# A mixer kernel's 3389 operations in a written-out order, in place of one derived from a list of priorities

## The chip, the cores and the metric

The program runs on one core of a Trainium2 chip. A core has a matmul engine (TensorE, PE in the profile, with its weight loads shown apart as PEld), three engines that work on tiles element by element (VectorE = DVE, ScalarE = ACT, GpSimd = POOL), and SyncE (SP), which here only issues transfers (DMAs). Each engine works through its own queue in order; engines wait for each other by semaphores. The metric is the device time of one execution in microseconds, lower being better; for each kernel the median of several runs.

## What is computed

Two kinds of layers alternate, A, B, A, B, over x of 2048 rows and 512 columns. The same weights serve both rounds.

```python
def _A_ref(x, wqkv, wo):                     # H = 32 heads of 16, window W = 8, dilation 2
    q, k, v = split(x @ wqkv)                # heads
    idx = pos[:, None] - off[None, :]        # off = 0, 2, ..., 14
    logits = einsum("bhsd,bhswd->bhsw", q, k[idx]) * scale     # idx < 0 masked
    o = einsum("bhsw,bhswd->bhsd", softmax(logits), v[idx])
    return merge(o) @ wo

def _B_ref(x, w1, w2, w3, w4):
    h = gelu(layernorm(x) @ w1)              # 512 -> 512
    hs = shift(h) @ w2                       # quarters of h shifted by +1, -1, +2, -2 rows
    x1 = x + hs
    return x1 + gelu(layernorm(x1) @ w3) @ w4        # 512 -> 1792 -> 512

x = x + _A_ref(layernorm(x), wqkv, wo)
x = x + _B_ref(layernorm(x), w1, w2, w3, w4)
x = x + _A_ref(layernorm(x), wqkv, wo)
x = x + _B_ref(layernorm(x), w1, w2, w3, w4)
```

## The kernel before

The 2048 rows are cut into four blocks of 512, each of four tiles of 128 rows; n = 0 to 7 counts the blocks of the first round (0 to 3) and of the second (4 to 7). For each n there are five stages:

- `p1_stream(n)` (for n = 0 `p1_quarters`) normalizes each tile, turns it (rows to columns, by `turn_pe`, four PE transposes, or `turn_dma`, one DMA transpose) and multiplies it with wqkv: per tile three blocks of 12 matmuls, whose results ACT copies to `ev` and SP stores to memory (`q_d`, `kv_d`).
- `p2(n)` is the attention in four units `qt` of eight heads. SP loads `q` and `kv` for it (unit n = 0 gets them by copies on the chip); DVE multiplies, reduces and adds the products (`prod`), POOL takes some of the additions.
- `p3(n)` multiplies with wo, adds to the residual tile `xs` (loaded by `load_res`), normalizes, turns, and multiplies with w1 (four blocks of 12), whose GELU goes to `h`.
- `p4(n)` multiplies with w2, adds, normalizes and turns again.
- `p5(n)` runs 14 chunks of the wide layer: w3 up to `mm`, GELU, w4 down into four accumulators `acc`. From n = 1 on each chunk loads a w3 and a w4 tile of 256 KB from memory into one of eight buffers `w`.

A matrix product is computed from 16-bit halves: each f32 operand is split into a high part (ACT, or POOL) and a rest (DVE), and three products are summed (`HLS`). The weights are scaled by a power of two from their sum of squares: `small_weight` does so for wo, w1 and w2 (load, a square on ACT, a small matmul with `ones` in `power_of`, a power on POOL), and `big_pair(c)` for a pair of chunks of w3 and w4, whose split halves are stored in memory for `p5`.

The program writes none of its instructions directly. Each step is an operation of a graph (`Graph.__call__`), made with the engines that may run it (`alts`: most have one, some two, such as DVE or POOL), planned durations, the buffers that it reads and writes, and the operations that must come before. An operation has a number, in the order in which it is made; `#2462` below is the operation with number 2462. At the end `plan` (line 265) puts all operations in one order, picks the engine of those that have a choice, and gives each buffer one of the places of its kind (`slots`: eight `w`, three `kv`, four `mm`, and so on). Then every operation is issued in this order, and `InOrder` keeps each engine's instructions in it. All instructions pass through one helper, so every row of the profile names line 385; rows are told apart by the names of tiles.

Before, `plan` is a simulation with a clock `now`. Whenever an engine is free, it starts the ready operation with the lowest key for which buffers are free:

```python
for e in (PE, ACT, DVE, POOL, SP):
    if free[e] > now or not ready[e]:
        continue
    ...
        it = heapq.heappop(ready[e])
        ...
        if all(sum(1 for s in pool[k] if s[0] <= now) >= m for k, m in need.items()):
            got = o
```

The key is the operation's entry in the list `PLACES`. An operation with two engines goes to the one that comes to it first.

## Time and profile before

| | |
|---|---|
| median of 3 runs | 1191.29 us (1185.78 to 1193.92) |
| the profiled execution | 1187.69 us |
| its span, first to last instruction | 1185.9 us |
| PE without an instruction in the span | 40.7 us |
| mean granted PE clock | 0.991 |

Rows of a timeline give the start in us from the span's start, the length, the engine, the operation with the tile written and the tiles read, the shape, the number of instructions merged into the row, and in brackets the engine's idle time before it and what ended it. Rows of stretches give, for each engine, the busy time and the number of instructions, then the granted PE clock, the share of the DMA engines and the GB/s. A matmul of 512 columns is shown as 0.38 us long, but its successor starts after 0.216 us: 12 of them take 2.6 us. `SPq` is SP's queue issuing a transfer; its length is not that of the transfer.

### The profile page before, as it was taken

What the parts mean: (1) busy time and instruction counts of PE and PEld (TensorE: products, weight loads), DVE (VectorE), ACT (ScalarE), POOL (GpSimd) and SP (SyncE); (2) the same over time, 40 slices, a digit from 0 to 9 for tenths busy, and PEclk for the clock granted to TensorE, in tenths of its full rate; (3) what the DMA queues carried; (4) which work ended last, traced back from release to release, by engine and by line L of the source; (5) the groups of instructions that cost most, each with busy time, mean ns of one, the idle gap of its engine ahead of it and who ended that gap; (6) DMA issues with size and microseconds to landing.
All of it is one profiled execution on the core that took longest, in us unless ns stands there. A gap on an engine that the chain in (4) does not pass through costs nothing.

```text
span 1185.9 us, 15311 instructions
## 1 busy us (share of the span) xinstructions
PE 1145.2 (97%) x5270; PEld 543.8 (46%) x5270; DVE 896.4 (76%) x1015; ACT 640.3 (54%) x1121; POOL 419.9 (35%) x568
## 2 busy tenths in 40 slices
PE   8989999999899989999999999999998999999998
PEld 6534444554344444444444444444343444444554
DVE  4789989998789989989877898269987789314122
ACT  5854577326865476555564467354644665445331
POOL 5443445004552345253641265031633352311000
PEclk9989999999999999999999999999999999999999
DMA  7565987877897685975578748578488765335222
GB/s 225 169 191 143 262 212 191 197 187 167 231 261 204 176 202 116 237 189 132 132 199 211 193 112 202 129 179 219 108 205 207 164 135 170 92 88 105 91 93 58
DMA packets 228046, 201.13 MB, mean 170 GB/s; under 512 B 109912, under 2 KB 171352, under 8 KB 227968
## 3 DMA queue, kind: packets, MB, share of 16 engines
q1 hardware_dynamic: 226352, 198.39, 65.3%
q10 hardware_dynamic: 1616, 1.77, 0.5%
q8 instruction: 41, 0.67, 0.2%
q14 instruction: 37, 0.30, 0.1%
HBM read 132.64 MB, written 37.87 MB: 144 GB/s over the span
## 4 chain that ended last, share of the span: by engine, by line
PE 75%; DVE 7%; DMA 7%; ACT 4%; SPq 3%; POOL 2%; issue 2%; DVEq 0%; ACTq 0%; POOLq 0%
PE mm L385 54%; PE acc L385 21%; DVE prod L385 4%; SPq L385 3%; DMA w<-w 2%; DVE L L385 1%; ACT junk L385 1%; POOL c L385 1%; DMA w<-in_B_w_dram 1%; ACT f L385 1%; DMA w<-in_A_x_dram 1%; POOL b L385 1%; DMA kv<-x 1%; DVE f L385 1%; DMA h<-in_B_w_dram 0%
## 5 line engine op out<-in xcount | busy, mean ns | idle before, releaser
L385 PE MATMUL mm<-nT,w 128*128 128x512 f16 (+1 forms) x1288 | 305.1, 390 | 7.9 <-DMA w<-w 4.9
L385 PE MATMUL acc<-w,g 128*128 128x512 f16 (+1 forms) x1260 | 308.2, 395 | 3.1 <-DMA w<-w 3.0
L385 PE MATMUL mm<-wq_hl,xt 128*128 128x512 f16 x1008 | 229.1, 384 | 4.3 <-DVE xt L385 2.2
L385 ACT ACTIVATE mm<-mm,s_w 128x512 f32<-128x512 f32 (+1 forms) x144 | 90.7, 630 | 207.9 <-PE mm L385 207.6
L385 PEld LDWEIGHTS <-w 128*128 128x128 f16 x1344 | 124.9, 98 | 148.3 <-DMA w<-w 6.8
L385 PEld LDWEIGHTS <-g 128*128 128x128 f16 x1176 | 115.4, 98 | 143.4 <-issue 7.3
L385 PEld LDWEIGHTS <-xt 128*128 128x128 f16 x1008 | 99.1, 99 | 124.5 <-issue 6.7
L385 DVE TENSOR_TENSOR prod<-kv,L 128x2048 f32<-128x2048 f32 x64 | 149.7, 2339 | 3.7 <-POOL o L385 1.8
L385 DVE TENSOR_TENSOR prod<-kv,q 128x2048 f32<-128x2048 f32 x58 | 137.8, 2376 | 13.1 <-DMA kv<-kv_d 7.6
L385 DVE TENSOR_REDUCE L<-prod 128x128 f32<-128x2048 f32 x64 | 145.6, 2276 | 0.2
L385 DVE TENSOR_TENSOR prod<-prod 128x1024 f32<-128x1024 f32 (+1 forms) x101 | 108.8, 1077 | 1.5
L385 DVE SCALAR_TENSOR_TENSOR g<-mm,c_g,g 128x512 f16<-128x512 f32 x56 | 41.8, 746 | 78.8 <-ACT g L385 78.7
L385 POOL TENSOR_TENSOR g<-f,g 128x512 f16<-128x512 f32 x32 | 44.0, 1378 | 145.0 <-ACT f L385 73.7
L385 PE MATMUL mm<-nT,w_hl 128*128 128x512 f16 x384 | 86.8, 379 | 5.2 <-ACT junk L385 3.1
L385 PE MATMUL mm<-w_hl,h 128*128 128x512 f16 x384 | 85.8, 379 | 0.0
L385 POOL TENSOR_TENSOR prod<-prod 128x512 f32<-128x512 f32 x33 | 47.3, 1432 | 102.8 <-DVE prod L385 102.6
L385 PE MATMUL mm<-wo_hl,oT 128*128 128x512 f16 x336 | 75.1, 379 | 0.0
L385 ACT ACTIVATE g<-mm,c_g 128x512 f16<-128x512 f32 x98 | 67.2, 686 | 2.1
L385 PEld LDWEIGHTS <-oT 128*128 128x128 f16 x426 | 41.5, 98 | 50.9 <-DVE oT L385 1.7
L385 POOL TENSOR_SCALAR b<-b 128x1 f32<-128x1 f32 (+1 forms) x48 | 22.8, 476 | 117.6 <-ACT junk L385 115.8
L385 ACT ACTIVATE ev<-mm,s_kv 128x512 f32<-128x512 f32 x56 | 38.2, 683 | 48.4 <-PE mm L385 44.6
L385 ACT ACT_TABLE_LOAD x46 | 59.0, 1283 | 4.1 <-issue 3.3
(205 smaller groups left out, 1385.5 us busy)
## 6 DMA issues: line engine op xcount, KB each, us to landing
w<-w SPq DMA_DIRECT2D x196, 256.0 KB
kv<-kv_d SPq DMA_DIRECT2D x112, 352.0 KB
w<-in_B_w_dram SPq DMA_DIRECT2D x56, 256.0 KB
kv_d<-ev SPq DMA_DIRECT2D x112, 128.0 KB
q_d<-ev SPq DMA_DIRECT2D x28, 256.0 KB
w<-g SPq DMA_DIRECT2D x28, 256.0 KB
q<-q_d SPq DMA_DIRECT2D x28, 256.0 KB
x<-x SPq DMA_DIRECT2D x26, 256.0 KB
```

The costliest lines, as they stand in the source:

```text
L385: i = f(*a, **k).ins
```

## The change

`PLACES` is now a permutation that says which place each operation has in one fixed order of all 3389, and a second list, `OTHER`, names the operations that run on the second of their engines. `plan` no longer chooses: it walks through the operations in this order and checks that each comes after those that it needs. It still computes planned times, but only to give a buffer the place that is planned to be free first. Nothing else differs: the operations, their tiles and the numbers of buffers are the same.

```diff
-import heapq
...
 PLACES = [int(k) for k in """
-627 626 619 617 724 832 135 355 315 730 540 1183 440 580 604 607 657 613 795 793 184 624 77 21
...
+103 2 7 0 1 179 3 4 11 10 17 8 18 9 20 25 51 46 36 37 5 6 14 15
...
 """.split()]
 
+OTHER = {int(k): 1 for k in """
+37 100 101 102 103 106 114 118 128 137 165 246 291 339 374 377 378 403 404 408 433 434 437 438
...
+2625 2629 2648 2757 2945 2955 2965 2975 3165
+""".split()}
...
 def plan(ops, slots):
-    free = list(FREE)
+    free, latest = list(FREE), {}
     lane, lanes = 0, [0.0] * LANES
     pool = {k: [(0.0, j) for j in range(len(v))] for k, v in slots.items()}
...
-    while left or fin:
...
-        for e in (PE, ACT, DVE, POOL, SP):
-            if free[e] > now or not ready[e]:
-                continue
...
+    for o in sorted(ops, key=lambda o: o.key):
+        assert o.n == 0, "an operation stands before one that it needs"
+        e, d, o.fn, cls = o.alts[OTHER.get(o.seq, 0)]
+        begin = o.est
+        for b in o.touch:
+            if b.slot is None:
+                got = min(pool[b.kind])
+                pool[b.kind].remove(got)
+                begin, b.slot = max(begin, got[0]), got[1]
+                b.t = slots[b.kind][b.slot]
+        begin = max(begin, free[e])
...
+        order.append(o)
...
+        for b in o.touch:
+            latest[b] = max(latest.get(b, 0.0), o.end)
+            b.left -= 1
+            if b.left == 0:
+                pool[b.kind].append((latest[b] + LAT, b.slot))
     return order
...
-    for _, _, o in plan(op.ops, slots):
+    for o in plan(op.ops, slots):
         o.fn()
```

The operations that the text names, with their new places in the order (lower comes first), are these:

| Engine | number (new place): what it is |
|---|---|
| PE | 494 (195), 90 (212), 497 (220): turn of a tile of `p1_stream(1)`, a block of `p1_quarters`, the first block on that turned tile |
| PE | 329 (243): the small matmul of `big_pair(6)`; 644 (254), 654 (257), 650 (258), 647 (276): turn of a tile of `p1_stream(2)` and its three blocks; 379 (269): turn of the first unit of `p2(0)`; 147 (277): w1's small matmul |
| PE | 1009 (569), 836 (570), 1013 (573): last turn of `p3(0)`, a block of `p1_stream(3)`, the first w1 block |
| PE | 1030 (607), 185 (618): a w1 block of `p3(0)`, the small matmul of `big_pair(0)` |
| PE | 858 (694), 1041 (695): a block of `p1_stream(3)`, the first turn of `p4(0)` |
| PE | 1232 (1127), 1373 (1153), 1237 (1161): last turn of `p4(1)`, a block of `p1_stream(4)`, the first w3 block of `p5(1)` |
| PE | 209 (988), 1352 (1008): the small matmul of `big_pair(1)`, a block of `p1_stream(4)` |
| ACT | 643 (245), 146 (271): normalization before 644, w1's square; 206 (987): a square of `big_pair(1)` |
| SP | 325 (241), 444 (250), 145 (253): a load of `big_pair(6)`, a copy of K for unit 3 of `p2(0)`, the load of w1 |
| SP | 201 (942), 205 (962), 1518 (983): two loads of `big_pair(1)`, a residual tile of `p3(2)` |
| SP | 1552 (1369): the last DMA transpose of `p3(2)` |
| SP | 2462 (2562), 2795 (2738): the w4 tile of chunk 11 of `p5(4)`, the w3 tile of chunk 5 of `p5(5)` |
| DVE | 375 (209): a product of the first unit of `p2(0)` |

Of the operations with a choice, 108 run on another engine than in the trace of before: 49 go from POOL to DVE and 30 from DVE to POOL (additions of `p2` and of the residual in `p4`), 14 from POOL to ACT and 9 from ACT to POOL (high parts and normalizations), 4 from ACT to DVE and 2 from DVE to ACT (squares at the start).

## The prediction

> **What bounds the kernel now.** I read the page first (busy shares and the chain that ended last), then the matmul engine's instructions in order of time with the idle time before each, then the stretches around the largest idle times.

> ```profile
> span 1185.9 us, 15311 instructions
> PE 1145.2 (97%) x5270; PEld 543.8 (46%) x5270; DVE 896.4 (76%) x1015; ACT 640.3 (54%) x1121; POOL 419.9 (35%) x568
> PE 75%; DVE 7%; DMA 7%; ACT 4%; SPq 3%; POOL 2%; issue 2%; DVEq 0%; ACTq 0%; POOLq 0%
> ```

> The reader is to see one engine that is never long without work: TensorE (PE) is busy for 1145.2 of 1185.9 us and carries three quarters of the chain. The change leaves every matmul as it is, so 1145.2 us of busy time stays, and what an order can win is at most the 40.7 us of PE idle time, and the time in which PE ran at half its clock. So I list the idle stretches and ask of each whether the new list removes it. The profiled execution took 1187.69 us, 3.6 below the median of the three runs (1191.29); the sum is made against 1187.69.

> **The change, part by part.** I sorted the operation numbers by their new places and set each engine's resulting order beside the order of the trace. No operation is added or dropped. PE's order hardly changes (498 operations, moved by 1.2 ranks on average); the other engines' orders change nearly everywhere (DVE by 13 ranks, POOL 15, SP 10, ACT 4).

> **a. Turn-rounds: PE waits for what it has just transposed.**

> ```profile
> 347.07 0.59 ACT L385 ACTIVATE nT<-mm 128x512 f16<-128x512 f32 x1
> 348.07 0.69 DVE L385 TENSOR_TENSOR nT<-mm,nT 128x512 f16<-128x512 f32 x1
> 347.71 0.59 PE L385 MATMUL mm<-nT,w 128*128 128x512 f16 x2 [0.83 <-ACT nT L385]
> 348.81 7.50 PE L385 MATMUL mm<-nT,w 128*128 128x512 f16 x34 [0.51 <-DVE nT L385]
> 65.45 0.61 PE L385 MATMUL mm<-wq_hl,xt 128*128 128x512 f16 x2 [0.76 <-ACT xt L385]
> 66.85 7.51 PE L385 MATMUL mm<-wq_hl,xt 128*128 128x512 f16 x34 [0.80 <-DVE xt L385]
> 123.02 5.34 PE L385 MATMUL mm<-wq_hl,xt 128*128 128x512 f16 x24 [1.37 <-DVE xt L385]
> 166.73 0.59 PE L385 MATMUL mm<-nT,w_hl 128*128 128x512 f16 x2 [0.93 <-ACT nT L385]
> 167.56 7.50 PE L385 MATMUL mm<-nT,w_hl 128*128 128x512 f16 x34 [0.24 <-DVE nT L385]
> 176.93 0.39 PE L385 MATMUL mm<-ss_p,ones 128*128 128x4 f32 x2 [0.85 <-ACT junk L385]
> 197.28 0.66 PE L385 MATMUL mm<-ident,f 128*128 128x128 f32 x4 [1.39 <-ACT f L385]
> ```

> Four transposes are split into a high part (ACT, 0.59) and a rest (DVE, 0.69), and a matmul that stands right behind them waits for both. Twelve matmuls of 512 columns last 2.6 us (34 in 7.50 here), more than ACT and DVE need. In the new list one such block stands in between at three of these places: #90 between #494 and #497 (0.76 + 0.80), #836 between #1009 and #1013 (0.93 + 0.24), #1373 between #1232 and #1237 (0.83 + 0.51). At 197.28 #858 stands ahead of #1041 and covers the 1.39; at 176.93 #185 moves behind #1030 (0.85). At 123.02 only a transpose of about 0.45 is put in between, so 0.45 of 1.37 goes. Sum: 1.56 + 1.17 + 1.34 + 1.39 + 0.85 + 0.45 = 6.8 us. What covers is PE's own work, which has to be done anyway and only moves; if its own inputs were late, the same wait would stand there. Bounds: 0 and 6.8. I take 6.8, for in the trace the inputs of #90 and #836 were there without a wait.

> **b. The load of w1.**

> ```profile
> 69.02 0.41 SPq L385 DMA_DIRECT2D h<-in_B_w_dram  x1
> 74.74 1.91 ACT L385 ACTIVATE w_hl<-h 128x2048 bf16<-128x2048 f32 x1 [2.56 <-DMA h<-in_B_w_dram]
> 76.79 0.38 PE L385 MATMUL mm<-ss_w,ones 128*128 128x1 f32 x2 [2.43 <-ACT w_hl L385]
> 78.07 1.11 PE L385 MATMUL mm<-ident,f 128*128 128x128 f32 x4 [0.90 <-ACT f L385]
> 92.00 0.66 PE L385 MATMUL mm<-ident,f 128*128 128x128 f32 x4 [0.78 <-ACT ev L385]
> 94.26 2.33 PE L385 MATMUL acc<-wo_hl,oT 128*128 128x512 f16 x10 [1.17 <-DVE oT L385]
> 70.00:90.00 20.00, 15.64 (x63) 6.87 (x61) 16.60 (x19) 12.24 (x21) 9.67 (x10) 0.83 0.80 226
> ```

> ACT stood for 2.56 us at the head of its queue for w1's square (#146); PE's #147 and ACT's next normalization, with the transposes #644 that need it, waited behind. The granted clock over 70 to 90 is 0.83, so 17% of 20 us, 3.4 us, was lost besides. The new list puts #643 ahead of #146 on ACT and #644, #654, #650, #379 and #647 ahead of #147 on PE. The idle rows of PE sum to 5.28 us, with the clock 8.7. But on SP the load (#145) now stands behind copies of K and V that wait for DVE (#444 among them), and #325, which PE's #329 needs, stands behind others; so a wait of the size of 2.43 may come again at #329. I keep it, and half of the clock: 0.90 + 0.78 + 1.17 + 1.7 = 4.6 us saved. Bounds: 0 and 8.7.

> **c. The squares of weight pair 1.**

> ```profile
> 298.90 1.12 SPq L385 DMA_DIRECT2D x<-in_A_x_dram  x2
> 300.12 0.53 SPq L385 DMA_DIRECT2D w<-in_B_w_dram  x1
> 309.10 0.39 PE L385 MATMUL mm<-ss_p,ones 128*128 128x4 f32 x2 [4.21 <-ACT junk L385]
> 306.00:316.00 10.00, 6.90 (x26) 2.93 (x27) 8.85 (x14) 9.67 (x20) 6.82 (x9) 0.83 0.79 203
> ```

> #209 waited 4.21 us for the square (#206) of a weight whose load SP issued late: SP stood until 298.90 for a residual tile (#1518), with the loads #201 (300.12) and #205 behind it. The clock of 0.83 over 10 us is 1.7 us more. In the new list #201 and #205 stand ahead of #1518, and #206 ahead of two other squares on ACT. PE's order there is the same. I expect #209 to come right behind the matmuls that end at 304.9, and the next stream (#1352), whose turned tile now is ready about 3 us earlier, some 0.8 us later: 4.21 + 1.7 - 0.8 = 5.1 us. Bounds: 0.9 (if SP's queue gives only what one issue takes) and 5.9.

> **d. Weight loads that came just in time.**

> ```profile
> 853.84 0.33 SPq L385 DMA_DIRECT2D w<-w  x1
> 856.48 9.53 PE L385 MATMUL acc<-w,g 128*128 128x512 f16 x36 [2.67 <-DMA w<-w]
> 909.28 0.38 SPq L385 DMA_DIRECT2D w<-w  x1
> 916.43 4.03 PE L385 MATMUL mm<-nT,w 128*128 128x512 f16 x12 [3.51 <-DMA w<-w]
> 910.00:925.00 15.00, 11.49 (x46) 4.70 (x45) 12.03 (x15) 9.04 (x13) 7.80 (x11) 0.89 0.68 176
> ```

> The w4 load #2462 was issued only when the matmuls right ahead of its user gave its buffer free, and PE waited 2.67 us; the w3 load #2795 had 5.2 us of matmuls between release and use, was issued behind copies on SP, and took 7.15 us (909.28 to 916.43) where the wait was 3.51. The clock of 0.89 over 15 us adds 1.7 there; at 856.48 the 36 matmuls took 9.53 where 34 took 7.50 above, 1.6 more than theirs. Counting matmuls between release and use, with the buffers handed out in the order in which they come free, the new list gives #2462 23 us and #2795 13 us; of the 196 such loads 35 had under 6 us, and 11 have it now. So 2.67 + 1.6 + 3.51 + 1.7 = 9.5 us. Bounds: 4.3 (only the first) and 9.5; 13 us is nearly twice the 7.15 that the slow one took.

> **e. The DMA transposes ahead of p3(2)'s w1.**

> ```profile
> 428.09 0.69 DVE L385 TENSOR_TENSOR prod<-f,prod 128x512 f16<-128x512 f32 x1 [0.52 <-ACT prod L385]
> 430.51 1.23 SPq L385 DMA_TRANSPOSE nT<-prod  x1
> 434.61 10.52 PE L385 MATMUL mm<-nT,w_hl 128*128 128x512 f16 x48 [3.11 <-ACT junk L385]
> ```

> The matmuls start 4.1 us after the issue of the transpose #1552 at 430.51, and its DVE half ended at 428.78, 1.7 us before the issue: SP stood at two other loads and a transpose. The new list moves those loads away from between the transposes. 1.6 of 3.11 us goes; the rest is the chain itself. Bounds: 0 and 1.7.

> **What is added.** 49 operations go from POOL to DVE and 30 the other way. What it costs DVE:

> ```profile
> L385 DVE TENSOR_TENSOR prod<-prod 128x512 f32<-128x512 f32 x35 | 26.4, 753 | 1.0
> L385 DVE TENSOR_TENSOR o<-prod 128x256 f32<-128x256 f32 x32 | 16.0, 501 | 4.7 <-POOL prod L385 3.8
> 350.00:720.00 370.00, 366.49 (x1697) 165.57 (x1695) 328.50 (x341) 213.43 (x340) 153.35 (x190) 1.00 0.70 175
> ```

> Net 11 adds of 512 columns in the sums of products, 1 of 256, and 7 of 512 in the residuals, at 0.753, 0.501 and again 0.753 us: some 14 us, 10 of them in 350 to 720, where DVE has 370 - 328.5 = 41.5 us without work. They lie beside PE's work, so I cost them at nothing; without that cover they would cost up to 14. Between POOL and ACT 14 operations go one way and 9 the other; ACT, busy 54%, hides them. The first and the last 6 places of PE's order are as before, so start and end keep their time.

> New waits are the unknown, for no trace shows them. Between none and those of b to e in before (8.7 + 5.9 + 9.5 + 3.1 us) I take nearest to the weaker end, since fewer loads are tight, and charge one at the price of the row of 916.43 with its clock, 3.51 + 1.7 = 5.2 us.

> Sum: 6.8 + 4.6 + 5.1 + 9.5 + 1.6 - 5.2 = 22.4 us, so 1187.7 - 22.4 = 1165.3 us.

> [...]

> **The rivals.**

> *POOL slows under DVE's adds.* Three small POOL steps of a statistic took 4.37 us here, from 70.75 to 75.11:

> ```profile
> 70.75 1.03 POOL L385 TENSOR_SCALAR a<-a 128x1 f32<-128x1 f32 x1 [6.27 <-ACT junk L385]
> 72.96 2.15 POOL L385 TENSOR_SCALAR a<-a,a 128x1 f32<-128x1 f32 x1
> 48.58 0.19 POOL L385 TENSOR_SCALAR a<-a 128x1 f32<-128x1 f32 x1
> ```

> The first took 1.03 where it took 0.19 at 48.58. If the denser DVE puts 3 us more on the statistics of five tiles that PE waits for, 15 us come back: 1180. Against it: POOL has 19 adds fewer. [...]

> *No change.* The waits are those of the chip's own spread and return elsewhere, 22.4 us more than I charge: 1187.7. For it: the waits c, d and the load in b hang on how fast loads land, which no order fixes. Against it: 6.8 us are turn-rounds, which are plain in the order, and 24 tight loads fewer.

> *Slower, by SP's queue.*

> ```profile
> 97.95 1.18 SPq L385 DMA_DIRECT2D kv<-x  x2
> ```

> #444 stands ahead of #145 on SP. It needs a K/V buffer; if it waits as long as in before (it was the second of these two issues, at 98.5), #145, behind it and two more issues, goes at about 100.5 in place of 69.02, and lands and is squared 7.6 us later (69.02 to 76.65): PE waits at #147 from about 84 to 108, 24 us and 3.4 of clock, and b is lost: 1165.3 + 24 + 3.4 + 4.6 = 1197.3. It is slower than before from an issue at about 89 us on. Against it: in the new list its buffer is freed by #375, a product of an earlier unit than the one that freed it in before.

> **How the numbers follow.** The forecast 0.62; POOL 0.14; no change 0.13; slower 0.06; better than the forecast's range (b in full, no new wait: 1165.3 - 4.1 - 5.2 = 1156.0, or less) 0.05. The likeliest is 1165.3. The range reaches from 1155 to 1183 (its own bounds and POOL's 1180, with 3 us for the spread of a median) and so takes in the forecast and POOL. A measurement of this kernel tells about 1% from no change, 1179.4 to 1203.2 against the median. Below it lie the forecast, the better case and half of POOL: 0.75; slower by over 1%, part of SP's case: 0.04; the rest, 0.21, within.

> **What would show it.** PE's idle time falls from 40.7 to about 20 us; no idle before the matmuls of #497, #1013, #1041 and #1237; #209 starts within 1 us of the matmuls ahead; no `<-DMA w<-w` over 1 us before PE; fewer stretches with a clock below 1. It is wrong if PE shows new waits of over 8 us in sum, or if DVE's products end later than p3 needs them, seen as PE waiting for `oT`.

## The result and the profile after

| kernel | median | profiled execution | its span | PE without an instruction |
|---|---|---|---|---|
| before, beside after | 1188.99 us (4 runs) | 1187.69 us | 1185.9 us | 40.7 us |
| after | 1158.3 us (4 runs, 1155.48 to 1160.68) | 1155.48 us | 1153.7 us | 19.2 us |

The ratio after to before is 0.9737, with a 95% interval of 0.9692 to 0.9783. The medians differ by 30.7 us, the two profiled executions by 32.2. The page of after, in the same three lines:

```profile
span 1153.7 us, 15248 instructions
PE 1134.5 (98%) x5270; PEld 540.9 (47%) x5270; DVE 893.6 (77%) x1038; ACT 641.9 (56%) x1122; POOL 353.3 (31%) x544
PE 84%; DVE 5%; DMA 5%; ACT 3%; SPq 2%; issue 1%; POOL 1%; POOLq 0%; DVEq 0%; ACTq 0%
```

The gain has two parts. PE's idle time fell by 21.5 us, from 40.7 to 19.2. PE's busy time fell as well, from 1145.2 to 1134.5, though its matmuls are the same: before ran them at half the clock (granted 0.50) in five stretches ahead of its tail (six units of 3.41 us, at 9.82, 78.09, 310.20, 856.33 and 917.77), after in none. Six such units cost at most 6 x 1.71 = 10.2 us of the 10.7.

PE's timeline of after, at the places of steps a to e (line L340 is the line that was L385 in before):

```profile
62.49 4.70 PE L340 MATMUL mm<-wq_hl,xt 128*128 128x512 f16 x21
72.53 0.60 PE L340 MATMUL mm<-wq_hl,xt 128*128 128x512 f16 x2 [0.69 <-ACT xt L340]
81.72 0.28 PE L340 MATMUL mm<-ss_w,ones 128*128 128x1 f32 x2
111.90 0.66 PE L340 MATMUL mm<-ident,f 128*128 128x128 f32 x4 [0.87 <-ACT f L340]
113.17 2.75 PE L340 MATMUL mm<-wq_hl,xt 128*128 128x512 f16 x12 [0.61 <-DVE xt L340]
116.54 3.83 PE L340 MATMUL mm<-wq_hl,xt 128*128 128x512 f16 x17 [0.62 <-ACT junk L340]
156.42 7.93 PE L340 MATMUL mm<-nT,w_hl 128*128 128x512 f16 x36
166.35 0.66 PE L340 MATMUL mm<-ident,prod 128*128 128x128 f32 x4 [1.99 <-ACT prod L340]
281.11 0.38 PE L340 MATMUL mm<-ss_p,ones 128*128 128x4 f32 x2 [0.85 <-ACT junk L340]
293.46 0.39 PE L340 MATMUL mm<-ss_p,ones 128*128 128x4 f32 x2 [1.02 <-ACT junk L340]
330.29 4.00 PE L340 MATMUL mm<-nT,w 128*128 128x512 f16 x17 [0.70 <-DVE nT L340]
414.06 6.21 PE L340 MATMUL mm<-nT,w_hl 128*128 128x512 f16 x28
828.67 7.50 PE L340 MATMUL acc<-w,g 128*128 128x512 f16 x34
852.69 3.63 PE L340 MATMUL mm<-wq_hl,xt 128*128 128x512 f16 x16 [0.76 <-DMA xt<-f]
886.37 2.75 PE L340 MATMUL mm<-nT,w 128*128 128x512 f16 x12
```

A row without a bracket had under 0.15 us of idle time ahead of it. #497 (62.49), #147 (81.72), #1013 (156.42), #1554 (414.06), #2463 (at 831.05, inside the row of 828.67) and #2796 (886.37) wait for nothing; in before they waited 1.56, 2.43, 1.17, 3.11, 2.67 and 3.51 us. #209 (293.46) still waits 1.02 of its 4.21. #1237 (330.29) still waits 0.70 of its 1.34. The waits at 281.11 (the small matmul of another weight pair) and 852.69 are new, that of 1.99 at 166.35 was 0.36 in before, and the three around 113 (2.10 in sum) replace one of 1.37.

The same timeline for ACT and SP shows what became of w1's load, of the transposes, and of two weight loads of step d (802.75 is #2788, and the first of the three at 817.65 is #2462):

```profile
69.58 0.48 SPq L340 DMA_DIRECT2D h<-in_B_w_dram  x1
76.24 1.91 ACT L340 ACTIVATE w_hl<-h 128x2048 bf16<-128x2048 f32 x1 [2.58 <-DMA h<-in_B_w_dram]
404.98 1.25 SPq L340 DMA_TRANSPOSE nT<-f  x1
406.32 1.27 SPq L340 DMA_TRANSPOSE nT<-prod  x1
407.69 3.69 SPq L340 DMA_TRANSPOSE nT<-f  x2
802.75 0.32 SPq L340 DMA_DIRECT2D w<-w  x1
817.65 1.30 SPq L340 DMA_DIRECT2D w<-w  x3
```

The load of w1 is no earlier (69.58 against 69.02), and ACT stands at it as long as before (2.58 against 2.56). But PE reaches #147 only at 81.72, when the square has long ended. The wait is still there, beside PE's work. Of the two weight loads, the one that is needed later (#2788, for 841.41) still goes out first; #2462, for 831.05, follows 14.9 us behind it and is now early enough.

### The profile page after: what moved, and what is told of

It reads as the page before. It is cut to its first block, busy times and chain, and to the rows that moved or that the text cites. A ratio compares the mean times of both kernels' runs of the same rounds, so it can differ in the third digit from the quotient of the medians.

```text
span 1153.7 us, 15248 instructions
## 1 busy us (share of the span) xinstructions
PE 1134.5 (98%) x5270; PEld 540.9 (47%) x5270; DVE 893.6 (77%) x1038; ACT 641.9 (56%) x1122; POOL 353.3 (31%) x544
## 3 DMA queue, kind: packets, MB, share of 16 engines
q10 hardware_dynamic: 1616, 1.77, 0.5%
## 4 chain that ended last, share of the span: by engine, by line
PE 84%; DVE 5%; DMA 5%; ACT 3%; SPq 2%; issue 1%; POOL 1%; POOLq 0%; DVEq 0%; ACTq 0%
PE mm L340 60%; PE acc L340 24%; DVE prod L340 2%; SPq L340 2%; DVE L L340 1%; POOL a L340 1%; DMA w<-w 1%; DMA w<-in_B_w_dram 1%; DMA w<-in_A_x_dram 1%; ACT junk L340 1%; DMA kv<-kv_d 1%; ACT f L340 1%; DMA prod<-in_A_x_dram 1%; DMA xt<-f 0%; DMA w<-g 0%
## 5 line engine op out<-in xcount | busy, mean ns | idle before, releaser
L340 PE MATMUL acc<-w,g 128*128 128x512 f16 (+1 forms) x1260 | 306.4, 393 | 0.0
L340 PE MATMUL mm<-nT,w 128*128 128x512 f16 (+1 forms) x1288 | 303.9, 388 | 2.0 <-ACT nT L340 0.7
L340 PE MATMUL mm<-wq_hl,xt 128*128 128x512 f16 x1008 | 226.2, 379 | 3.1 <-DVE xt L340 1.1
L340 ACT ACTIVATE mm<-mm,s_w 128x512 f32<-128x512 f32 (+1 forms) x144 | 90.0, 627 | 185.9 <-PE mm L340 185.5
L340 PEld LDWEIGHTS <-w 128*128 128x128 f16 x1344 | 124.7, 98 | 142.4 <-DMA w<-w 2.1
L340 PEld LDWEIGHTS <-g 128*128 128x128 f16 x1176 | 114.9, 98 | 137.7 <-issue 0.3
L340 PEld LDWEIGHTS <-xt 128*128 128x128 f16 x1008 | 98.2, 98 | 120.0 <-issue 2.0
L340 DVE TENSOR_TENSOR prod<-kv,L 128x2048 f32<-128x2048 f32 x64 | 147.0, 2297 | 4.7 <-POOL o L340 3.7
L340 DVE TENSOR_REDUCE L<-prod 128x128 f32<-128x2048 f32 x64 | 145.9, 2280 | 0.8
L340 DVE TENSOR_TENSOR prod<-kv,q 128x2048 f32<-128x2048 f32 x58 | 136.1, 2349 | 11.0 <-DMA kv<-kv_d 5.4
L340 DVE TENSOR_TENSOR prod<-prod 128x1024 f32<-128x1024 f32 (+2 forms) x114 | 115.4, 1012 | 2.8
L340 PE MATMUL mm<-nT,w_hl 128*128 128x512 f16 x384 | 86.6, 379 | 0.3 <-DVE nT L340 0.2
L340 DVE SCALAR_TENSOR_TENSOR g<-mm,c_g,g 128x512 f16<-128x512 f32 x56 | 41.4, 743 | 58.4 <-ACT g L340 58.1
L340 PE MATMUL mm<-w_hl,h 128*128 128x512 f16 x384 | 86.0, 379 | 0.0
L340 POOL TENSOR_TENSOR g<-f,g 128x512 f16<-128x512 f32 x35 | 49.2, 1407 | 109.2 <-ACT f L340 52.1
L340 POOL TENSOR_TENSOR o<-prod 128x256 f32<-128x256 f32 x31 | 24.5, 790 | 173.6 <-DVE prod L340 153.2
L340 PE MATMUL mm<-wo_hl,oT 128*128 128x512 f16 x336 | 75.6, 379 | 0.0
L340 ACT ACTIVATE g<-mm,c_g 128x512 f16<-128x512 f32 x98 | 66.4, 684 | 1.9
L340 ACT ACTIVATE ev<-mm,s_kv 128x512 f32<-128x512 f32 x56 | 38.0, 681 | 49.2 <-PE mm L340 36.4
L340 PEld LDWEIGHTS <-oT 128*128 128x128 f16 x426 | 41.6, 98 | 50.3 <-issue 1.7
L340 POOL TENSOR_TENSOR prod<-prod 128x512 f32<-128x512 f32 x19 | 26.8, 1412 | 105.0 <-DVE prod L340 101.5
```

The source lines that it names most:

```text
L340: i = f(*a, **k).ins
```

## The experiments

All of them use the form of after, a fixed list, and edit the list or the engines. The order of before, written out as such a list, gives every buffer the same place as before's own rules do; an edit of the list can change places behind it, and no run holds them fixed. Ratios are to before on the same chip, whose median lay between 1187.8 and 1189.4 us in all runs; differences to after compare medians. The lead of one kernel over another is how much earlier it does the same matmuls, in us, read from the two profiles. In the edits below, numbers are operations in the order of their engine.

### The steps done alone, in the order of before

**Turn-rounds (step a).** Only PE's order is edited, at five places (two are shown; with #1373 go the copy of its result on ACT and a transfer on SP):

```diff
-PE: ... 662 90 494 497 ...  995 836 1002 1009 1013 ...
+PE: ... 662 494 90 497 ...  995 1002 1009 836 1013 ...
```

> The order of before, with nothing changed but the turn-rounds on the matmul engine: #90 behind #494, #836 behind #1009, #1373 behind #1232, #858 ahead of #1041, #185 behind #1030 (step a of the prediction). Theory 1 (the prediction): the swaps on the matmul engine are the gain, 1.56 + 1.17 + 1.34 + 1.39 + 0.85 = 6.3 us, and the five waits are gone. Theory 2: the swaps need inputs that stand ready, and in before only some do. The input of #494 ends at 62.87 in before, and without #90 the engine is there at 61.5, so it waits 1.4 there; #1231 ends at 345.11, and the engine is there at 343.7; #858 needs the same turned tile that ends at 197.26. Then only #1009 (1.17) and #185 (0.85) are won and about 1 us is lost at the other places: 0 to 2 us in all, within 0.2% of before.

Measured: 1194.56 us, ratio 1.0049 (1.0028 to 1.0069), slower than before. At the first place, PE's timeline is:

```profile
62.34 0.65 PE L340 MATMUL mm<-ident,f 128*128 128x128 f32 x4 [1.44 <-ACT f L340]
62.92 2.85 PE L340 MATMUL mm<-h,g 128*128 128x384 f32 x8
66.96 5.22 PE L340 MATMUL mm<-wq_hl,xt 128*128 128x512 f16 x22 [1.20 <-ACT xt L340]
```

#494 waits 1.44 us for its input, as theory 2 said, and #497 still waits 1.20, because ACT, whose order is unchanged, comes late to the turned tile. Theory 1 falls: a block put between a turn and its user covers a wait only where the turn itself could start earlier. Theory 2 expected a small gain and missed too: of the five waits only those of #1041 and #185 are gone, #1013 waits 2.04 (1.17 in before) and #1237 1.98, and two other turns wait 1.48 and 1.26 where they had no wait.

**Loads (steps c, d, e).** Only SP's order is edited:

```diff
-SP: ... 1518 201 296 255 205 ...  1528 1618 1536 1648 1544 1623 1552 ...
+SP: ... 201 296 255 205 1518 ...  1528 1536 1544 1552 1623 1648 1618 ...
-SP: ... 2788 ... 2462 ...  2810 ... 2795 ...
+SP: ... 2462 ... 2788 ...  2795 ... 2810 ...
```

> The order of before, with nothing changed but the DMA issues of SP at three places: the loads #2462 and #2788 change places, and #2795 and #2810 (step d: in before a load that was needed 14 to 25 us later got the free buffer first); #1518 behind #205 (step c); the three weight loads that stood between the transposes behind #1552 (step e). The prediction: d 9.5, c 5.1, e 1.6 us, 16.2 in sum. Theory 2: d gives its 9.5, for both loads then go out 7 to 10 us earlier; c gives nothing, since the buffer of #205 came free only at 302.07 in before and ACT works without a pause from 301 to 309, where #206 stands behind three others; e gives 1.6. That is 11.1 us, and the wait before #209 stays at about 4.

Measured: 1189.88 us, ratio 1.0011 (0.9992 to 1.003): no gain beyond the noise, where the prediction had 16.2 and theory 2 had 11.1. PE's timeline, and one row of SP's:

```profile
312.56 0.59 PE L340 MATMUL mm<-ss_p,ones 128*128 128x4 f32 x2 [4.21 <-ACT junk L340]
436.40 10.52 PE L340 MATMUL mm<-nT,w_hl 128*128 128x512 f16 x48 [0.71 <-DMA nT<-prod]
449.79 1.63 PE L340 MATMUL mm<-wq_hl,xt 128*128 128x512 f16 x5 [2.87 <-DMA xt<-f]
856.73 10.52 PE L340 MATMUL acc<-w,g 128*128 128x512 f16 x48
871.05 5.16 PE L340 MATMUL mm<-nT,w 128*128 128x512 f16 x17 [3.79 <-DMA nT<-f]
919.00 2.75 PE L340 MATMUL mm<-nT,w 128*128 128x512 f16 x12
305.56 0.33 SPq L340 DMA_DIRECT2D w<-in_B_w_dram  x1
```

Each move does at its own place what was expected: the waits of 2.67 (#2463, inside the row of 856.73) and 3.51 (919.00) are gone, and that of 3.11 is down to 0.71. #209 waits 4.21 as before: #205 went out 7.0 us ahead of #209's start (305.56 against 312.56), as in before (302.09 against 309.10), since a step on DVE gave its buffer free no earlier. And new waits took the place of the old ones. PE stands at #1554 for 0.71 only and, one block of 10.5 us later, runs into a transposed tile of `p1_stream(5)` that is ready no earlier (its transpose went out when DVE's half of the tile ended, at 443.52): 2.87 at 449.79, where before had 0.11. It no longer stands at #2463, and runs into the end of `p4(5)`, whose four transposes are no earlier either: 3.79 at 871.05. Behind both PE was slower besides: the five matmuls at 449.79 took 1.63 us, where five that start 0.216 apart take 1.24, and the 17 at 871.05 took 5.16, where in after a row of 17 took 4.00 (330.29); the mean granted clock of this profile is 0.987, of before's 0.991. In before these two chains were as late, and the earlier waits had hidden it.

**w1's square (step b, and the ACT side of c).**

```diff
-ACT: ... 397 146 501 643 505 645 ...  1363 256 1186 206 ...
+ACT: ... 397 643 146 501 505 645 ...  206 1363 256 1186 ...
-PE:  ... 504 147 644 647 650 ...
+PE:  ... 504 644 647 147 650 ...
```

> The order of before, with nothing changed but the square of w1 (step b) and the square #206 (the ACT side of step c): on ACT #643 ahead of #146, on the matmul engine #147 behind #647; on ACT #206 ahead of three others. The prediction put b at 4.6 us with all of the change (bounds 0 and 8.7), and c at 5.1 with SP and ACT together. Theory 2: #643 waits for its statistic, which ended at 75.11 in before, so the wait at #147 only moves to #644: about 2.0 us are won at 80, and 3.4 more only if the stretches at half clock (78.09 to 84.92) go as well; the rest of b comes from the statistic being early, which this kernel does not change. #206 comes 1.6 us earlier, and the wait before #209 falls from 4.21 to about 2.6. In sum 3.6 us, or 7.0 to 8.7 with the clock.

Measured: 1188.11 us, ratio 1.0004 (0.9984 to 1.0024). The rows:

```profile
73.69 1.91 ACT L340 ACTIVATE w_hl<-h 128x2048 bf16<-128x2048 f32 x1 [1.76 <-DMA h<-in_B_w_dram]
78.09 0.59 ACT L340 ACTIVATE xt<-mm 128x512 f16<-128x512 f32 x1
78.74 4.28 PE L340 MATMUL mm<-wq_hl,xt 128*128 128x512 f16 x12 [4.89 <-ACT xt L340]
```

Theory 2 was wrong about the cause: #643 did not wait for a statistic (its own, #642, had ended by 46 us), and #644 ran at 73.25. But the next link, the split #645 (78.09), still stood behind the square on ACT, so the whole wait moved to #647: 4.89 us. The #206 side gave 1.19 of #209's 4.21 (3.02 left), and the next matmul waited 1.15 in turn.

**The whole chain of step b.** The edit above without #206, and with #645 ahead of #146 as well, on DVE #646 ahead of #332, on PE #147 behind #650.

> The order of before, with step b made on all three engines that its chain runs through: on ACT #643 and #645 ahead of the square #146 that waits for w1, on DVE #646 ahead of #332, on the matmul engine #147 behind #650. The run with #643 alone moved the wait to #645, which still stood behind #146. Theory: #647 starts at about 75 in place of 79.88, and the stretch at half clock at 78.09 goes: 5 + 3.4 = 8.4 us are won by 90 us (the whole of step b, which the prediction put at 4.6). If the gain is kept to the end, the median is 1180; if later chains are in step with the old times, most of it comes back as longer waits behind 90 us, and the median is 1185 or above.

Measured: 1184.92 us, ratio 0.998 (0.996 to 1.0001), not told apart from no change. #650, the second block of the turned tile, was 5.3 us ahead of before (79.67 against 84.95), and then:

```profile
77.08 5.34 PE L340 MATMUL mm<-wq_hl,xt 128*128 128x512 f16 x24 [1.41 <-DVE xt L340]
86.60 1.09 PE L340 MATMUL mm<-ident,o 128*128 128x128 f32 x4 [4.06 <-ACT ev L340]
84.31 0.63 ACT L340 ACTIVATE junk<-w 128x512 bf16<-128x512 f32 x1 [1.73 <-DMA w<-in_A_x_dram]
85.79 0.67 ACT L340 ACTIVATE ev<-mm,s_q 128x512 f32<-128x512 f32 x1
```

PE's next turn needs one of the four `mm` buffers, which ACT empties (`ev<-mm`), and that step stands on ACT behind a square that waits for the next load (1.73 us at 84.31). 4.06 us are given back at once: one step waiting for a load at the head of ACT's queue is passed, and the next one stands there.

**The adds alone.** The order of before, the 79 adds on their new engines.

> The order of before; of the change only the 79 adds between POOL and DVE stand on their new engines. With them put back, the order of after lost 17.5 us, for an add on POOL that waited for a product of DVE stood ahead of the statistic of a normalization. Theory 1 (the moves are worth as much by themselves): 10 us or more are won, 1179 or below. Theory 2 (the places and the engines belong together; in the order of before the adds on POOL stand where nothing urgent is behind them): within 5 us of before, 1184 to 1194, with the large waits at 76.79, 309.10, 434.61, 856.48 and 916.43 still there.

Measured: 1190.67 us, ratio 1.0015 (0.9996 to 1.0034). Theory 2 holds: the waits stand at 2.82 (#147), 4.23 (#209), 2.79 (#1554) and 2.65 (#2463); only that of #2796 was shorter, 1.23.

### The change with one part put back

**Turn-rounds put back.** PE's order of after, with #90, #836, #1373 and #185 moved forward and #858 moved back.

> The order of after, with the turn-rounds on the matmul engine put back as in before (#90 ahead of #494, #836 ahead of #1002, #1373 ahead of #1212, #858 behind #851, #185 ahead of #1030). Theory 1 (the prediction): the waits come back, 6.3 us more than after. Theory 2: what is won in after is that inputs come earlier, and the swaps matter where a turned tile is needed at once: 1.56 at #497 and 1.17 at #1013 come back; at #1041 the input ended at 185.24 in after, ahead of the engine, so nothing comes back there; at #1237 DVE ends at 330.84 in any case, so nothing; 2.7 to 3.6 us in all.

Measured: 1164.37 us, ratio 0.9792 (0.9755 to 0.9828), 6.1 us above after's median; the intervals of the two ratios overlap a little. The sum is theory 1's, the places are not: #497 waits 1.41 again and #1013 0.98, #1041 nothing (there theory 2 is right), #185 1.88 where before had 0.85, and #1237 waits 2.02; behind it 26 matmuls took 7.54 us, where in after 28 took 6.21 (414.06).

**SP put back.** With the issues, a few steps of PE, ACT and DVE had to move by some places.

> The order of after on the matmul engine, DVE, ACT and POOL, with the DMA issues of SP in the order of before, wherever that can be (77 issues had to stand elsewhere, because of buffers; the mean place is 0.7 from that of before, 9.1 from that of after). Theory 1 (the prediction put 16.2 us on the order of the loads, steps c to e): about 1158.3 + 16.2 = 1174.5, with waits for w, or for the squares of weights, of over 2 us before the matmul engine. Theory 2: the loads alone gained nothing in the order of before, so what counts is the order of ACT, DVE and POOL, by which buffers come free and chains end: within 5 us of after.

Measured: 1446.62 us, ratio 1.218 (1.2133 to 1.2227). Neither theory comes near. What PE and SP's queue waited for most:

```profile
PE mm L340 <- DMA w<-w: 59.1, 18, 8.6
PE acc L340 <- DMA w<-w: 31.7, 9, 14.4
SPq L340 <- ACT ev L340: 196.2, 33, 16.6
```

(Total us, times, longest; the third line is 51.4, 26 and 5.6 in after.) Where a copy of a result stands ahead of a load on SP's queue, and ACT now produces that result later than in the old order, the load waits with it, up to 16.6 us. Here the old order of transfers did not fit the new order of what makes them. Of the 288 us that it costs, PE's waits for weight tiles (`w<-w`) are 91, and PE's longer busy time 75 (1209.4 us in place of 1134.5, at a mean granted clock of 0.930 in place of 0.999); the rest was not taken apart.

**Engines put back**, all of them, then the adds and the rest apart. The list of places is that of after.

> The order of after, with every operation on the engine of before (the 49 adds and others go back from DVE to POOL, the 30 from POOL to DVE, and so on). The prediction costed the moves at nothing (hidden beside the matmul engine): within 2 us of after, 1156 to 1160. Rival 1: DVE with 14 us less to do ends its steps earlier, 3 us or more are gained. Rival 2: the new order counts on the faster engine at places where a chain ends late (an add of 512 columns takes 0.75 us on DVE), so 4 us or more come back, seen as waits for DVE or POOL.

Measured: 1191.92 us, ratio 1.0028 (1.0012 to 1.0044): the whole gain is gone. Rival 2, and eight times its price.

> The order of after; of the engine choices only the 79 adds between POOL and DVE (49 and 30) are put back to those of before. The prediction costed them at nothing: within 2 us of after (1156 to 1160). Rival: in the run with all engines as before, the lead fell from 14 us behind at 25 us to 37 us behind at the end; if the adds are what cost the 23 us behind the start, this kernel loses 10 us or more, with the matmul engine waiting for steps that come behind a slow add on POOL.

Measured: 1175.83 us, ratio 0.99 (0.9879 to 0.9921), 17.5 us above after. The largest new wait, in the timelines of POOL, ACT and PE:

```profile
278.05 0.74 POOL L340 TENSOR_TENSOR o<-prod 128x256 f32<-128x256 f32 x1 [5.54 <-DVE prod L340]
278.87 2.29 POOL L340 TENSOR_SCALAR b<-b 128x1 f32<-128x1 f32 x1
281.25 1.53 POOL L340 TENSOR_TENSOR b<-b,nhalf 128x1 f32<-128x1 f32 x1
282.88 0.35 POOL L340 TENSOR_SCALAR b<-b,b 128x1 f32<-128x1 f32 x1
283.26 0.81 ACT L340 ACTIVATE f<-x,b,b 128x512 f32<-128x512 f32 x1 [5.47 <-POOL b L340]
284.13 0.91 PE L340 MATMUL mm<-ident,f 128*128 128x128 f32 x4 [3.90 <-ACT f L340]
```

It is read from the top. The add #728 stands at the head of POOL's queue and waits 5.54 us for a product of DVE. Behind it stand the three small steps of #1150, a statistic, then ACT's normalization #1151 with it, then PE's turn #1152. Nobody waits for the add here; ACT and PE wait for what is queued behind it. In before the add was on POOL too, but one place behind #1150. In after it stands ahead of it in the list (886 against 889) and on DVE, where it holds up nothing on POOL. What costs at this place is not that POOL is slower (0.74 us for this add, where DVE's 32 of this size took 0.50 on average in before), but what stands behind it. The place explains 3.9 of the 17.5 us, and slower matmuls right behind it about 1.5 (six in 4.22 us at 284.83, where six ahead of the wait took 2.74 at 277.50); the rest is spread over waits that grew by at most 1.5 us each.

> The counterpart: the order of after; of the engine choices only the 29 that involve ACT (#22 of the first normalization, six squares of the first weights, ten high parts of weights and others) are put back to those of before. In the run with all engines as before, #22 ended at 11.73 in place of 7.38, since it stood behind other work on POOL, and the squares #103 and #106 ended 12 us later on ACT. Theory: 12 to 18 us more than after (1170 to 1176), all of it ahead of 45 us. Rival (start is hidden by what comes later): under 5 us.

Measured: 1172.96 us, ratio 0.9873 (0.9849 to 0.9898), 14.7 us above after, and 14.1 us of lead are lost by 25 us in the profile, as the theory said. One row of POOL and one of PE:

```profile
11.37 0.76 POOL L340 TENSOR_SCALAR f<-w,a,a 128x512 f32<-128x512 f32 x1
12.19 1.12 PE L340 MATMUL mm<-ident,f 128*128 128x128 f32 x4 [5.78 <-POOL f L340]
```

The first normalization starts on POOL at 11.37 (on ACT at 6.57 in after), behind the statistic of another tile, and PE waits 5.78 us for it. The two parts add up: 17.5 + 14.7 = 32.2 of the 33.6 us that all the engines put back cost. After itself leads before by only 1.5 us at 24 us; so these choices do not win 14 us against before, they spare the new order a loss.

### The change in one stretch

> The first 1375 places (to the first matmul of w1 in p3(2), at 414 us in after) as in after, the rest in the order and on the engines of before. In the traces after led before by 20.5 us there, and by 32.2 at the end. Theory A (the gain of a stretch stands by itself): 20.5 us less than before, about 1167.5. Theory B (a gain is kept only if what follows is in step, as the single moves suggest, whose waits came back at the next load or chain): the lead shrinks behind the cut, by 8 us or more, to 1176 or above.

Measured: 1178.33 us, ratio 0.9916 (0.9892 to 0.994): 10.8 us, theory B.

> The counterpart: the first 1375 places in the order and on the engines of before, the rest as in after. Theory A: what after gains behind the cut, 32.2 - 20.5 = 11.7 us, so about 1176.5. Theory B: the late loads and chains of the first part meet the new order, and under 4 us are gained. If the gains of this kernel and of its counterpart sum to about 30 us, stretches add up.

Measured: 1176.1 us, ratio 0.9898 (0.9868 to 0.9928): 13.0 us, theory A's number. The two sum to 23.8 of 30.7. What is missing shows in the first of them at the seam:

```profile
438.99 6.17 PE L340 MATMUL mm<-wq_hl,xt 128*128 128x512 f16 x17 [7.79 <-DMA xt<-prod]
433.51:443.75 10.24, 4.76 (x12) 1.73 (x13) 9.20 (x8) 2.27 (x4) 3.36 (x6) 0.50 0.64 173
```

One transposed tile comes 7.79 us late, and three clock units (row of the stretch; the number behind the instruction counts is the granted clock, 0.50) run at half speed: the lead over before's profile falls from 14.2 us at 445 to 4.0 at 460. This profile is the slowest of ten executions (1185.64 us, 7.3 above the median), and ahead of the seam it had already lost 6.6 us of after's lead, with a wait of 2.03 us for a load at 227.44 that after does not have. So the loss at the seam is shown, but not its size in a median execution. A long stretch of the new order keeps 11 to 13 us.

## Why the prediction was right, and where its steps failed

The predicted 1165.3 us is 7.0 above the measured 1158.3 and the range holds it. The list of waits that go was right nearly throughout: of the signs that it named, #1237 missed with 0.70 us of idle time left and #209 with 1.02 in place of under 1. The reason given for them was not: it took each wait for a step that is worth its price by itself, and no step tried alone made the kernel faster beyond the noise. The sum came near because the listed waits did go together; that it came near for a reason that does not hold is luck.

| step | predicted | measured in after against before |
|---|---|---|
| a, turn-rounds | 6.8 | 4.9: the six waits fell from 7.67 to 2.80 |
| b, load of w1 | 4.6 | 7.2: idle 5.28 to 1.50, clock 3.4 |
| c, weight pair 1 | 5.1 | 4.9: 4.21 to 1.02, clock 1.7 |
| d, two late loads | 9.5 | 9.2: the lead grew from 22.6 at 851 to 31.8 at 923, with 0.76 lost at 852.69 in it |
| e, transposes | 1.6 | 3.1: all of it |
| new waits outside d | -5.2 | -2.5: 1.6 more at 166.35, 0.85 at 281.11, no clock |
| the start | 0 | 1.5 |
| load waits of 0.3 to 1.0 in before | 0 | about 2 |

That makes 30.3 of 32.2; the rest lies in waits of under 0.9 us.

- **a.** "What covers is PE's own work, which has to be done anyway and only moves" failed as a reason. Alone, PE's swaps made the kernel 6.7 us slower. #1041's wait of 1.39 stays away in after even with PE's swap undone, for ACT's #1040 is early.
- **b.** "A wait of the size of 2.43 may come again at #329" failed: #329 waits 0.05, since #325 still went out at 65.13, 5 us ahead of PE's need. The clock went whole, not by half. The rival with #444 on SP's queue fell: it was issued at 67.03 and #145 at 69.58.
- **c.** The size was right, the cause was not. With SP's order alone #209 waits 4.21 as before, for DVE gives #205's buffer free only 2.8 us before PE is ready for #209 (302.07 against 304.89 in before). The residual tile #1518 could hold back only #201, by 2.2 us (buffer free at 297.90, issued at 300.12). In after DVE gives #205's buffer free 6.6 us before (285.85 against 292.44). With ACT's side alone 3.02 are left. So DVE's places seem to count beside SP's and ACT's; this is not shown, for no run tries the three together without the rest.
- **d.** Right in mechanism and size: in after #2462's buffer is free 23.1 us ahead of its user and #2795's 12.8, as counted. The two swaps in the run with the loads alone are another cure, which after does not use: before gave the free buffer to the load with the later user, and so does after (#2788 ahead of #2462, and #2810, issued at 852.40 for 891.55, ahead of #2795, at 877.71 for 886.37). Made alone, the second swap kept its gain, and the first lost it again at 871.05, to the chain behind it.
- **e.** "The rest is the chain itself" failed. The bound of 1.7 counted only the last transpose's delay; loads stood between all four. Moving just these loads takes 2.40 of 3.11.
- **What is added.** "So I cost them at nothing" failed most. DVE's load is indeed hidden (busy 893.6 us, 896.4 in before). But the moves also decide what waits at the head of POOL's and ACT's queues, and with engines put back the new order is worth nothing.
- **New waits, 5.2.** Over-sized: 2.5 came, and 0.76 inside d. This term, b and e are 6.8 of the 9.8 us that lie between 22.4 and 32.2.

*POOL slows under DVE's adds* fell: the 96 statistics on POOL took 152.3 us in before and 147.8 in after, and PE's longest wait for POOL in after is 0.36 us. (In before DVE did run an add of two tiles, from 70.71 to 71.40, beside the slow step that the prediction shows, and nothing beside the fast one at 48.58; two steps do not show a cause.) *No change* was the fate of every step tried alone but a, which was slower; it was not that of the whole. (The chance of 0.75 for a time below 1179.4 adds up to 0.74.)

What stays open: which of the many differing places on DVE, ACT and POOL make the new order hold together. The runs show that none of the steps tried does it alone, that SP and the engines must fit the rest, and that a part of the program in the new order keeps 11 to 13 us. The new compute order with the old SP order was tried, the reverse was not; nor were the choices that involve ACT alone in the old order, or any kernel with the places of the buffers held fixed.

## What to carry to other kernels

Where one engine is 97% busy and every other one runs in order, a wait in the profile can be, as here, the latest of several chains that are nearly as late; removing it alone then uncovers the next (2.87 and 3.79 us in the run with the loads alone), so before costing it, look at how much later than its user each of the following inputs comes. When an operation changes engine, cost what stands behind it in the queue that it leaves and in the one that it joins, above all if it waits there for a third engine; its own duration is the small part (0.74 us of POOL, where PE waited 3.90, in the run with the adds put back). Look at how long ahead of its user a load's buffer comes free: giving it to the load whose user comes first removed both waits in the old order, though no time was gained by it alone, and the new order frees buffers earlier instead. Keep steps that wait for a load from the head of a queue that has urgent work behind it (a wait of 1.73 us for a load on ACT came with one of 4.06 on PE).

## What the runs showed of the hardware

```profile
852.92:856.33 3.41, 0.89 (x5) 0.29 (x3) 3.41 (x4) 1.41 (x3) 2.70 (x3) 1.00 0.23 77
856.33:859.74 3.41, 3.26 (x8) 1.14 (x8) 3.32 (x7) 3.11 (x6) 1.44 (x3) 0.50 0.19 40
429.66:433.08 3.42, 1.83 (x9) 0.63 (x7) 3.42 (x6) 0.48 (x2) 0.00 (x0) 1.00 1.12 248
433.08:436.49 3.41, 1.88 (x9) 0.90 (x10) 3.41 (x8) 3.31 (x9) 2.05 (x7) 1.00 1.32 294
436.49:439.90 3.41, 3.41 (x18) 1.56 (x16) 2.83 (x6) 3.38 (x5) 2.51 (x6) 1.00 0.69 197
```

The wait of 2.67 us ahead of 856.48 lay nearly all in one unit (2.52 us idle), and the next ran at 0.50. The wait of 3.11 us ahead of 434.61 fell on a boundary, 1.58 and 1.53, and the clock stayed at 1.00. So the shorter of these two waits cost clock, and the longer did not. In all of before, six units at 1.00 had 2.07 to 3.01 us of idle time (those from 6.41, 74.68, 306.78, 852.92, 914.36 and, in the tail, 1180.60), and each was followed by one at 0.50; the unit with the next most, 1.89 (from 303.37), was not, nor was any with less. In after no unit ahead of the tail had more than 1.69 (from 162.64), and none was followed by one at 0.50. Before was back at 1.00 behind units at 0.50 with 0.00 to 0.48 us of idle time; the unit at 78.09, with 0.69, was followed by a second at 0.50. These are counts from two executions; where a limit lies, or whether it is a sharp one, they do not show, and no kernel was made to test it.

Some waits repeat to 0.01 us in the five profiled kernels with before's order at these places (before, and the runs of loads, of w1's square, of the whole chain of b and of the adds alone): #1013 1.17 and #1041 1.39, ended by ACT or DVE. Others do not: #497, ended by ACT and DVE, 1.39 to 1.77, and #2796, which waits for a load, 1.23 to 3.51 in the four of them in which its load was not edited.
